# A list scheduler that keeps VectorE's SBUF operations off GpSimd's additions, with new due times and another order of products in the first full round

## The chip, the cores and the metric

One core of one Trainium2 chip. The metric is the time of one execution on the device, in microseconds; of several runs the median.

## The reference

Softcapped attention, then a feed-forward layer with an ELU between its two products. Cut to what matters:

```python
# q, k, v: (4, 12, 448, 64); cap = 30; w_in: (768, 2048), w_out: (2048, 768), both float64
scores = cap * tanh((q @ k.T / 8) / cap)
attn = exp(scores - max) / (sum + 1e-9)
x = (attn @ v).transpose(0, 2, 1, 3).reshape(1792, 768)
h = x @ w_in
g = where(h > 0, h, exp(min(h, 0)) - 1)
out = (g @ w_out).astype(float32)
```

## The kernel before, in words

The attention (Attention.run, the first 155 us) runs over 12 rounds of two pairs of heads, in an order written out by hand; the change does not touch it. Its result x stays in SBUF as 6 chunks c of 128 features by 1792 tokens.

The layers run over 8 rounds r. A round takes 256 of the 2048 hidden features, as two slices f = 2r and 2r + 1, and the tokens in four blocks t: 384, 384, 512 and 512 wide (BLOCKS, L33). Every operand is split in a high and a low part of a rounded format; a product is then three matrix multiplies (high by high, low by high, high by low: products, L398, lines L402 to L404). Names in the trace and the order: xh1_3 and xl1_3 are the two parts of block 1, chunk 3; wh7 and wl7 those of weight tile 7; h2_0 is slice 2 of block 0 in PSUM, e2_0 its ELU on the way, gh2_0 and gl2_0 the parts of the result; o0_3_2 the output of round 0, block 3, chunks 2 and 3.

Blocks 0 and 1 go through h (hidden, 18 multiplies a slice) and o (outputs, 12 multiplies for each pair of chunks, three pairs). For blocks 2 and 3 the first product of rounds 1 to 7 is not made directly: seven products m1 to m7 of half the depth (block, 9 multiplies each) take the place of eight, on sums and differences of quarters of the weights and of x ("forms"; the x ones are kept in DRAM and fetched into a ring of three SBUF slots, t1_3_0 and so on). VectorE's additions (add, L489 to L497) and ScalarE's copy (keep) put the seven together in SBUF as c1, c, u2 and u3, and each gives one h. Round 0 makes all four blocks directly.

PSUM: two single banks hold h and m in turn, three double ones ("s") hold o. A bank is free again when the operation that reads it has run: for h the bend (L435, VectorE, of the ELU: exp on ScalarE L430 and L431, bend, high part on ScalarE L445, low part on VectorE L449); for m the keep or the add; for o in round 0 the leave (ScalarE, L467), later the gather (VectorE, L472), which adds o to x.

The weights come as float64 words, one tile of 128 by 768 at a time, four tiles a round (4r and 4r + 1 for h and m, 4r + 2 and 4r + 3 for o). Weights.steps makes each one a float32 out of its bits: ScalarE L118 and L121, VectorE L129, L132 and L145, GpSimd's integer addition (L148), ScalarE's high part (L155), VectorE's low part (L159). The load of a tile into its one buffer (L106) waits for L145 of the tile before.

The order of all this is made while the program is built. Each operation is a Step with an engine, a length in us from a formula, a due time, what it needs, gives, takes and frees; steps stand in threads, and Plan.run places them one at a time: the engine that can start first, and on it, of the steps that can start then, the one with the smallest due time. TensorE's steps are one thread in a fixed order (plan_products), and Moe.clock adds up their lengths: due times are given against that clock. The result is only an order for each engine; on the chip every engine takes its list in that order and waits for semaphores.

Of the kernel before, what the change touches and what calls it, by code (L numbers as in the profile page):

```python
# [18 lines left out]
BANK = 512  # L19
# [6 lines left out]
FT = 2  # L26
# [274 lines left out]
class Step:  # L301


    def __init__(self, engine, us, due, f, *a, needs=(), gives=None, takes=None, frees=()):
        self.engine, self.us, self.due, self.f, self.a = engine, us, due, f, a
        self.needs, self.gives, self.takes, self.frees = needs, gives, takes, frees


class Plan:
# [31 lines left out]
    def run(self):  # L341

        free, order = dict(FREE), []
        heads = [[t, 0, -9.0] for t in self.threads]
        while heads:
            able = []
            for head in heads:
                step = head[0][head[1]]
                start = self.ready(step, head[2])
                if start is not None:  # L350
                    able.append((start, step, head))
            first = {}
            for start, step, head in able:
                e = step.engine
                start = start if e is None else max(start, free[e])
                first[e] = min(first.get(e, start), start)
            if not first:
                raise RuntimeError([h[0][h[1]].a for h in heads])
            engine = min(first, key=lambda e: first[e])
            now = first[engine]  # L360
            due, _, step, head = min(
                ((step.due, k, step, head) for k, (start, step, head) in enumerate(able)
                 if step.engine == engine and start <= now),
                key=lambda e: e[:2],
            )
            end = now + step.us
            if engine is not None:
                free[engine] = end
            order.append(step)
            end += LAG[engine]  # L370
            if step.takes is not None:
                kind, owner = step.takes
                self.slots[kind][1].append(None)
                self.owner[owner] = kind, len(self.slots[kind][1]) - 1
            for owner in step.frees:
                kind, k = self.owner.pop(owner)
                self.slots[kind][1][k] = end
            if step.gives is not None:
                self.known[step.gives] = end
            head[1] += 1  # L380
            if head[1] == len(head[0]):
                heads.remove(head)
            else:
                head[2] = now + step.us if head[0][head[1]].engine == engine else end
# [5 lines left out]
class Moe:  # L390
# [121 lines left out]
    def plan_elu(self, r, t, i, due, needs=(), frees=(), freed=()):  # L512
# [4 lines left out]
            Step("v", dve(width), due + 1.2, self.bend, *k, frees=frees, gives=freed or None),  # L517
            Step("s", act(width), due + 2.5, self.high, *k, takes=("g", ("g", *k))),
            Step("v", dve(width), due + 4.0, self.low, *k, frees=(("e", *k),), gives=("g", *k)),
        )  # L520

    def plan_first(self, r, t, i):
# [9 lines left out]
        self.plan_elu(r, t, i, end, needs=(("p", r, t, i),), frees=frees)  # L532

    def plan_second(self, r, t):
# [3 lines left out]
        for e in range(0, NC, 2):  # L538
            single = last and e == NC - 2
            for k in (e, e + 1) if single else (e,):  # L540
# [6 lines left out]
                if r:  # L547
                    step = Step("v", dve(n * width), end + 1.5, self.gather, r, t, k, n, needs=(key,), frees=(key,))
# [7 lines left out]
    def plan_block(self, n, r):  # L556
# [26 lines left out]
        if n == 1:  # L583
            p.thread(
                Step("s", act(BANK), end, self.keep, "c1", "m1", r, needs=(key,), frees=(key,),
# [4 lines left out]
        more = {}  # L590
        if out == "c":
            more["takes"] = "ev", ("c", r)
        elif out:
# [3 lines left out]
        add = [Step("v", dve(BANK), end, self.add, u, f"m{n}", r, out, needs=needs, gives=gives,  # L597
                    frees=() if n == 5 else (key,), **more)]
        if n == 5:
            add.append(Step("v", dve(BANK), end, self.add, "u2", "m5", r, gives=("u", "u2", r, 5), frees=(key,)))  # L600
# [3 lines left out]
        for name, t, i, ready in elu:  # L604
            got = ("got", name, r)
            p.thread(Step(None, 0.0, 0.0, self.bring, name, r, t, i, needs=(ready,), gives=got))
            self.plan_elu(r, t, i, end + 0.8, needs=(got,), frees=((name, r),))

    def plan_products(self):
# [6 lines left out]
        self.plan_elu(0, 0, 0, -2.4, needs=(("p", 0, 0, 0),))  # L616
# [6 lines left out]
        for r in range(1, NR):  # L623
            self.begun[r] = self.clock
            for n in (1, 6):
                if r == 1 and n == 1:
                    first(r, 0)
                self.plan_block(n, r)
            if r > 1:
                first(r, 0)  # L630
            self.plan_second(r - 1, 3)
            self.plan_block(7, r)
            first(r, 1)
            self.plan_second(r, 0)
# [107 lines left out]
    def run(self, normalised):  # L742
# [14 lines left out]
        for r in range(1, NR):  # L757
            start = self.begun[r]
            before = self.begun.get(r - 1, start - 56.0)
            for i in range(FT):  # L760
                self.plan_tile(2 * FT * r + i, (before + 12.0 if r > 1 else start - 24.0) + 13.0 * i)
            self.plan_forms(r, before + 34.0 if r > 1 else start - 4.0)
            for i in range(FT, 2 * FT):
                self.plan_tile(2 * FT * r + i, before + 13.0 * i + 12.0 if r > 1 else start + 10.0 * (i - 1) - 4.0)
# [3 lines left out]
class Attention:  # L768
# [225 lines left out]
    def plan_rest(self, p):  # L994
# [6 lines left out]
        def spread(k, *needs):  # L1001
# [11 lines left out]
            Step("v", 0.7, 0.0, self.take_sums, n, needs=("summed",), frees=(("sums",),)),  # L1013
            Step(None, 3.7, 0.0, None),
            Step("v", 0.32, 0.0, self.invert, n),
# [244 lines left out]
```

## Time and profile before

| | |
|---|---|
| median of 3 runs | 622.81 us (622.63 to 626.21) |
| the profiled execution's own time | 623.72 us |
| its span, first to last instruction | 621.9 us |
| TensorE (PE) busy | 608.4 us, 98% of the span |
| VectorE (DVE) busy | 491.0 us, 79% |
| ScalarE (ACT) busy | 365.3 us, 59% |
| GpSimd (POOL) busy | 63.7 us, 10% |
| TensorE's granted clock, mean | 0.997 of full speed |

Busy time is the union of an engine's instructions; a matrix multiply is shown longer than the distance to the next one, since they overlap, so distances from start to start tell TensorE's pace. A row of the timeline shows start and length in us, engine, line, operation and operands; a bracket at its end shows how long the engine was idle before it and what ended that.

### The profile page before, as it was taken

The numbers are of one execution on the slowest core, as the hardware profiler recorded it, in microseconds if no ns is written. First come the engines' busy times: TensorE is split into PE (matmuls) and PEld (weight loads), VectorE is DVE, ScalarE is ACT, GpSimd is POOL, SyncE is SP. The second block draws the span as 40 slices with busy tenths as digits, with TensorE's granted clock in tenths as the row PEclk, the third lists the DMA queues.
The fourth block names the chain that finished last, engine by engine and source line by source line (L and its number), as shares of the span: only waits on it lengthen the run. The fifth ranks groups of instructions, "written<-read, shape, count | busy, mean of one in ns | idle before, by whom it ended". The sixth has DMA issues, their size and how long they took to land.

```text
span 621.9 us, 8936 instructions
## 1 busy us (share of the span) xinstructions
PE 608.4 (98%) x3347; PEld 473.6 (76%) x3347; DVE 491.0 (79%) x684; ACT 365.3 (59%) x527; POOL 63.7 (10%) x40
## 2 busy tenths in 40 slices
PE   8999999999999989899999999999999999999996
PEld 3444444444798879788988998898889889888985
DVE  5898999997899957986895989588688959764463
ACT  6999999999866954644453544345454434431330
POOL 0010010010110122112111101111111112010000
PEclk9999999999999999999999999999999999999999
DMA  5556457462222875644544444454644445342444
GB/s 186 166 162 208 130 151 232 128 208 59 84 82 85 338 237 201 237 143 146 207 168 169 156 149 159 155 199 168 229 152 157 153 153 203 110 170 85 163 168 174
DMA packets 39622, 103.08 MB, mean 166 GB/s; under 512 B 11026, under 2 KB 15890, under 8 KB 39570
## 3 DMA queue, kind: packets, MB, share of 16 engines
q1 hardware_dynamic: 39282, 101.90, 48.0%
q8 instruction: 28, 0.46, 0.3%
q10 hardware_dynamic: 288, 0.52, 0.3%
q14 instruction: 24, 0.20, 0.1%
HBM read 90.44 MB, written 11.88 MB: 165 GB/s over the span
## 4 chain that ended last, share of the span: by engine, by line
PE 87%; DVE 7%; DMA 2%; ACT 2%; issue 1%; SPq 0%; DVEq 0%; ACTq 0%
PE o L404 11%; PE o L402 11%; PE o L403 11%; PE pv L853 10%; PE s L811 8%; PE m L402 5%; PE m L404 5%; PE m L403 5%; PE h L402 5%; PE h L403 5%; PE h L404 5%; PE sum L897 3%; PE pv L866 2%; PE s L828 1%; DVE xl L248 1%
## 5 line engine op out<-in xcount | busy, mean ns | idle before, releaser
L402 PE MATMUL o<-gh,wh 128*128 128x384 f32 (+1 forms) x380 | 138.2, 364 | 1.8 <-ACT wv L118 1.8
L404 PE MATMUL o<-gh,wl 128*128 128x384 f32 (+1 forms) x380 | 138.4, 364 | 0.0
L403 PE MATMUL o<-gl,wh 128*128 128x384 f32 (+1 forms) x380 | 138.0, 363 | 0.0
L472 DVE TENSOR_TENSOR x<-o,x 128x768 f32<-128x768 f32 (+1 forms) x83 | 89.8, 1084 | 22.6 <-PE o L404 22.0
L148 POOL TENSOR_TENSOR wv<-wv,wq 128x768 int32<-128x768 int32 x24 | 47.3, 1973 | 362.6 <-DVE wv L145 322.9
L402 PEld LDWEIGHTS o<-gh,wh 128*128 128x128 f32 x380 | 71.7, 189 | 9.9 <-ACT wv L118 2.2
L844 ACT ACTIVATE s<-s 128x896 f32<-128x896 f32 x84 | 76.6, 912 | 4.6 <-PE s L828 3.5
L846 ACT ACTIVATE p<-s 128x896 f32<-128x896 f32 x84 | 77.2, 919 | 2.7
L403 PEld LDWEIGHTS o<-gl,wh 128*128 128x128 f32 x380 | 71.7, 189 | 7.9
L404 PEld LDWEIGHTS o<-gh,wl 128*128 128x128 f32 x380 | 71.6, 189 | 7.7
L402 PE MATMUL h<-xh,wh 128*128 128x384 f32 (+1 forms) x210 | 71.4, 340 | 0.8 <-DVE e L435 0.8
L404 PE MATMUL h<-xh,wl 128*128 128x384 f32 (+1 forms) x210 | 71.2, 339 | 0.0
L403 PE MATMUL h<-xl,wh 128*128 128x384 f32 (+1 forms) x210 | 71.2, 339 | 0.0
L853 PE MATMUL pv<-p,vf 128*64 128x448 f32 x276 | 59.5, 552 | 0.0
L445 ACT ACTIVATE gh<-e 128x384 fp32r<-128x384 f32 (+1 forms) x64 | 36.0, 570 | 27.1 <-DVE e L435 27.1
L430 ACT ACTIVATE e<-h 128x384 f32<-128x384 f32 (+1 forms) x36 | 18.0, 499 | 54.8 <-PE h L404 54.7
L435 DVE SCALAR_TENSOR_TENSOR e<-e,h 128x384 f32<-128x384 f32 (+1 forms) x36 | 20.2, 564 | 34.4 <-ACT e L431 34.3
L449 DVE TENSOR_TENSOR gl<-e,gh 128x384 fp32r<-128x384 f32 (+1 forms) x64 | 41.0, 650 | 6.7 <-ACT gh L445 6.7
L402 PEld LDWEIGHTS h<-xh,wh 128*128 128x128 f32 x210 | 39.4, 188 | 3.9 <-DVE e L435 1.1
L853 PEld LDWEIGHTS pv<-p,vf 128*64 128x64 f32 x276 | 16.8, 136 | 31.0 <-issue 23.3
L403 PEld LDWEIGHTS h<-xl,wh 128*128 128x128 f32 x210 | 39.4, 188 | 1.3
L404 PEld LDWEIGHTS h<-xh,wl 128*128 128x128 f32 x210 | 39.4, 188 | 0.7
(132 smaller groups left out, 1036.5 us busy)
## 6 DMA issues: line engine op xcount, KB each, us to landing
t<-form SPq DMA_DIRECT2D x81, 512.0 KB, 5.3
pre<-in_w_dram SPq DMA_DIRECT2D x32, 768.0 KB, 5.7
raw<-in_qk_dram SPq DMA_DIRECT2D x22, 448.0 KB, 4.2
form<-t SPq DMA_DIRECT2D x12, 512.0 KB, 3.9
vf<-in_v_dram SPq DMA_DIRECT2D x23, 256.0 KB, 4.4
rb<-rec SPq DMA_DIRECT2D x48, 112.0 KB, 2.9
out_dram<-x SPq DMA_DIRECT2D x5, 512.0 KB, 2.8
out_dram<-x SPq DMA_DIRECT2D x6, 384.0 KB, 2.5
```

The costliest lines, as they stand in the source:

```text
L148: nc.gpsimd.tensor_tensor(out=vi, in0=vi, in1=q, op=ALU.add)
L402: mm(acc, wh[:, m, :], ph, start=first, stop=False)
L403: mm(acc, wh[:, m, :], pl, start=False, stop=False)
L404: mm(acc, wl[:, m, :], ph, start=False, stop=last)
L435: self.nc.vector.scalar_tensor_tensor(out=e, in0=e, scalar=-1.0, in1=self.h.pop(k), op0=ALU.add, op1=ALU.max)
L445: self.nc.scalar.activation(out=self.g[k][0], in_=self.e[k], func=AF.Copy)
L449: self.nc.vector.tensor_tensor(out=gl, in0=self.e.pop(k), in1=gh.bitcast(F32), op=ALU.subtract)
L472: self.nc.vector.tensor_tensor(out=o, in0=self.o.pop((r, t, e)), in1=o, op=ALU.add)
L811: yield lambda a=a, b=b, i=i: self.nc.tensor.matmul(s, a[o, k], b[o, :S], start=i == 0, stop=i == 2)
L844: self.nc.scalar.activation(out=s, in_=s, func=AF.Tanh, scale=self.con.tanh_scale)
L846: self.nc.scalar.activation(out=pt, in_=s, func=AF.Exp, scale=self.con.exp_scale)
L853: self.nc.tensor.matmul(out[o, :S], w[j], x[j], **flags)
```

## The change

Four things.

- Step gets a flag psum. A VectorE step without it (one on SBUF alone) and a GpSimd step exclude each other in the plan: Plan.run lets neither start before the other engine's last such step has ended (held). Steps with the flag are the bends of h, the adds that read m, the gathers, and the sums and their reciprocal. The order of instructions is all that comes of it; no wait is added to the program.
- The due times of the ELU, the adds and the keep move ahead: the exp of an h from the end of its product to 3 us before it, the bend from 1.2 us behind the exp to the same time, the high and low part from 2.5 and 4.0 to 3.0 and 4.5 us behind; adds and keep to 3 us before their product's end; the sums of the last attention round to -9.
- In round 1, o of round 0's block 3 stands ahead of m1 and m6 instead of behind them, and m7 behind h of block 1 instead of ahead of it.
- The due times of the weight tiles and of the weight forms are given against the start of their own round: the add of tiles 4r to 4r + 3 at -32, -19, +2 and +13, the forms at -14 (all 4 later in round 1).

```diff
-    def __init__(self, engine, us, due, f, *a, needs=(), gives=None, takes=None, frees=()):
+    def __init__(self, engine, us, due, f, *a, needs=(), gives=None, takes=None, frees=(), psum=False):
+        self.other = None if psum else {"v": "g", "g": "v"}.get(engine)
...
+        held = {"v": -9.0, "g": FREE["g"]}
...
-                start = start if e is None else max(start, free[e])
+                start = start if e is None else max(start, free[e], held.get(step.other, start))
...
-                 if step.engine == engine and start <= now),
+                 if step.engine == engine and max(start, held.get(step.other, start)) <= now),
...
             if engine is not None:
                 free[engine] = end
+                if step.other is not None:
+                    held[engine] = end
...
-    def plan_elu(self, r, t, i, due, needs=(), frees=(), freed=()):
+    def plan_elu(self, r, t, i, due, needs=(), frees=(), psum=True):
...
-            Step("v", dve(width), due + 1.2, self.bend, *k, frees=frees, gives=freed or None),
-            Step("s", act(width), due + 2.5, self.high, *k, takes=("g", ("g", *k))),
-            Step("v", dve(width), due + 4.0, self.low, *k, frees=(("e", *k),), gives=("g", *k)),
+            Step("v", dve(width), due, self.bend, *k, frees=frees, psum=psum),
+            Step("s", act(width), due + 3.0, self.high, *k, takes=("g", ("g", *k))),
+            Step("v", dve(width), due + 4.5, self.low, *k, frees=(("e", *k),), gives=("g", *k)),
...
-        self.plan_elu(r, t, i, end, needs=(("p", r, t, i),), frees=frees)
+        self.plan_elu(r, t, i, end - 3.0, needs=(("p", r, t, i),), frees=frees)
...
-                    step = Step("v", dve(n * width), end + 1.5, self.gather, r, t, k, n, needs=(key,), frees=(key,))
+                    step = Step("v", dve(n * width), end + 1.5, self.gather, r, t, k, n, needs=(key,), frees=(key,),
+                                psum=True)
...
-                Step("s", act(BANK), end, self.keep, "c1", "m1", r, needs=(key,), frees=(key,),
+                Step("s", act(BANK), end - 3.0, self.keep, "c1", "m1", r, needs=(key,), frees=(key,),
...
-        add = [Step("v", dve(BANK), end, self.add, u, f"m{n}", r, out, needs=needs, gives=gives,
-                    frees=() if n == 5 else (key,), **more)]
+        due = end - 3.0
+        add = [Step("v", dve(BANK), due, self.add, u, f"m{n}", r, out, needs=needs, gives=gives,
+                    frees=() if n == 5 else (key,), psum=True, **more)]
...
-            self.plan_elu(r, t, i, end + 0.8, needs=(got,), frees=((name, r),))
+            self.plan_elu(r, t, i, end, needs=(got,), frees=((name, r),), psum=False)
...
-        self.plan_elu(0, 0, 0, -2.4, needs=(("p", 0, 0, 0),))
+        self.plan_elu(0, 0, 0, -3.5, needs=(("p", 0, 0, 0),))
...
         for r in range(1, NR):
             self.begun[r] = self.clock
+            if r == 1:
+                first(r, 0)
+                self.plan_second(r - 1, 3)
             for n in (1, 6):
-                if r == 1 and n == 1:
-                    first(r, 0)
                 self.plan_block(n, r)
             if r > 1:
                 first(r, 0)
-            self.plan_second(r - 1, 3)
-            self.plan_block(7, r)
+                self.plan_second(r - 1, 3)
+                self.plan_block(7, r)
             first(r, 1)
+            if r == 1:
+                self.plan_block(7, r)
             self.plan_second(r, 0)
...
         for r in range(1, NR):
             start = self.begun[r]
-            before = self.begun.get(r - 1, start - 56.0)
-            for i in range(FT):
-                self.plan_tile(2 * FT * r + i, (before + 12.0 if r > 1 else start - 24.0) + 13.0 * i)
-            self.plan_forms(r, before + 34.0 if r > 1 else start - 4.0)
-            for i in range(FT, 2 * FT):
-                self.plan_tile(2 * FT * r + i, before + 13.0 * i + 12.0 if r > 1 else start + 10.0 * (i - 1) - 4.0)
+            first = 0 if r > 1 else 4.0
+            for i, due in enumerate((-32.0, -19.0, 2.0, 13.0)):
+                if i == FT:
+                    self.plan_forms(r, start + first - 14.0)
+                self.plan_tile(2 * FT * r + i, start + first + due)
...
-            Step("v", 0.7, 0.0, self.take_sums, n, needs=("summed",), frees=(("sums",),)),
+            Step("v", 0.7, -9.0, self.take_sums, n, needs=("summed",), frees=(("sums",),), psum=True),
             Step(None, 3.7, 0.0, None),
-            Step("v", 0.32, 0.0, self.invert, n),
+            Step("v", 0.32, 0.0, self.invert, n, psum=True),
```

How the order of instructions changes is shown at three places; behind each fence stands what moved.

First, VectorE between the attention's last tile (wv3) and block 1. num23 is a copy out of PSUM; e0_0 with h0 is the bend of the first half of h0; sums11 the last softmax sums; xl1_0 and so on the low parts of block 1. Before:

```order
L904 COPY num23_1874<-pv11_1_1822 128x448
L248 TENSOR_TENSOR xl1_0_1808<-x_123,xh1_0_1807 128x384
L248 TENSOR_TENSOR xl1_1_1810<-x_123,xh1_1_1809 128x384
L248 TENSOR_TENSOR xl1_2_1812<-x_123,xh1_2_1811 128x384
L435 SCALAR_TENSOR_TENSOR e0_0_1896<-e0_0_1896,h0_1841 128x384
L248 TENSOR_TENSOR xl1_3_1814<-x_123,xh1_3_1813 128x384
```

And in the change:

```order
L912 COPY num23_1874<-pv11_1_1822 128x448
L439 SCALAR_TENSOR_TENSOR e0_0_1896<-e0_0_1896,h0_1841 128x384
L917 TENSOR_SCALAR sums11_1909<-sum11_1876,eps_88 128x448
L248 TENSOR_TENSOR xl1_0_1808<-x_123,xh1_0_1807 128x384
L248 TENSOR_TENSOR xl1_1_1810<-x_123,xh1_1_1809 128x384
```

The bend and the sums stand ahead of the low parts now.

Second, VectorE in round 1, up to the first gather of o1_1: c1 and u2 are the sums that take in m2 and m3, wv and wl a weight tile, forms the weight forms of round 2. Before:

```order
L145 SCALAR_TENSOR_TENSOR wv10_2736<-pre_73,wv10_2736 128x768
L497 TENSOR_TENSOR c1_1_2478<-c1_1_2478,m2_1_2713 128x512
L211 TENSOR_TENSOR forms_1889<-pre_73,forms_1889 128x384
L211 TENSOR_TENSOR forms_1889<-wv9_2656,forms_1889 128x384
L211 TENSOR_TENSOR forms_1889<-pre_73,forms_1889 128x384
L435 SCALAR_TENSOR_TENSOR e2_2_2791<-e2_2_2791,c1_1_2478 128x512
L497 TENSOR_TENSOR u2_1_2515<-u2_1_2515,m3_1_2732 128x512
L449 TENSOR_TENSOR gl3_2_2771<-e3_2_2723,gh3_2_2770 128x512
L449 TENSOR_TENSOR gl2_2_2815<-e2_2_2791,gh2_2_2814 128x512
L159 TENSOR_TENSOR wl10_2810<-wv10_2736,wh10_2809 128x768
L472 TENSOR_TENSOR x_123<-o1_1_0_2752,x_123 128x2x384
```

And in the change:

```order
L145 SCALAR_TENSOR_TENSOR wv9_2701<-pre_73,wv9_2701 128x768
L501 TENSOR_TENSOR u2_1_2553<-u2_1_2553,m3_1_2726 128x512
L476 TENSOR_TENSOR x_123<-o1_1_0_2743,x_123 128x2x384
L439 SCALAR_TENSOR_TENSOR e2_2_2735<-e2_2_2735,c1_1_2530 128x512
L453 TENSOR_TENSOR gl3_2_2757<-e3_2_2716,gh3_2_2756 128x512
L159 TENSOR_TENSOR wl9_2776<-wv9_2701,wh9_2775 128x768
L453 TENSOR_TENSOR gl2_2_2781<-e2_2_2735,gh2_2_2780 128x512
```

The gather of o1_1_0 stands right behind the add of m3; tile 9 is at that place where tile 10 was, and the forms come later.

Third, ScalarE before o1_0: wh7 is the high part of weight tile 7, which o1_0 reads, x<-o0_3 are the leaves of round 0's block 3, e2_1 and e3_1 the exponentials of h2_1 and h3_1. Before:

```order
L467 ACTIVATE x_123<-o0_3_0_2500 128x2x512
L467 ACTIVATE x_123<-o0_3_2_2524 128x2x512
L155 ACTIVATE wh7_2558<-wv7_2517 128x768
L467 ACTIVATE x_123<-o0_3_4_2544 128x2x512
L118 ACTIVATE pre_73<-pre_73 128x768
L121 ACTIVATE wq8_2580<-pre_73 128x768
L430 ACTIVATE e2_1_2611<-h2_1_2576 128x384
```

And in the change:

```order
L118 ACTIVATE wv7_2555<-pre_73 128x768
L121 ACTIVATE wq7_2563<-pre_73 128x768
L434 ACTIVATE e2_1_2579<-h2_1_2544 128x384
L435 ACTIVATE e2_1_2579<-e2_1_2579 128x384
L449 ACTIVATE gh2_1_2598<-e2_1_2579 128x384
L434 ACTIVATE e3_1_2608<-h3_1_2574 128x384
L435 ACTIVATE e3_1_2608<-e3_1_2608 128x384
L155 ACTIVATE wh7_2617<-wv7_2555 128x768
```

Tile 7's first steps and its high part move behind the leaves of block 3, and the high part behind the exponentials of h3_1.

## Rows read from the trace of the kernel before

**Rows 1.** Waits of TensorE, 148 us to the end: total, times, longest (us).
```profile
PE o L402 <- ACT wv L118: 1.8, 1, 1.8
PE m L402 <- issue: 1.7, 1, 1.7
PE m L402 <- DVE e L435: 1.2, 1, 1.2
PE h L402 <- DVE e L435: 0.8, 1, 0.8
```

**Rows 2.** Timeline of TensorE around the four waits: start, length, line, operands.
```profile
162.59 0.34 PE L404 MATMUL h<-xh,wl 128*128 128x384 f32 x1
163.76 0.45 PE L402 MATMUL h<-xh,wh 128*128 128x384 f32 x1 [0.83 <-DVE e L435]
...
215.35 0.34 PE L404 MATMUL h<-xh,wl 128*128 128x384 f32 x1
216.91 0.50 PE L402 MATMUL m<-xh,wh 128*128 128x512 f32 x1 [1.21 <-DVE e L435]
...
220.98 0.47 PE L402 MATMUL m<-t,forms 128*128 128x512 f32 x1 [1.74 <-issue]
...
260.28 0.39 PE L404 MATMUL m<-t,forms 128*128 128x512 f32 x1
262.48 0.47 PE L402 MATMUL o<-gh,wh 128*128 128x512 f32 x1 [1.81 <-ACT wv L118]
...
266.43 0.40 PE L403 MATMUL o<-gl,wh 128*128 128x512 f32 x1
...
269.87 0.39 PE L403 MATMUL o<-gl,wh 128*128 128x512 f32 x1
```

**Rows 3.** Busy time by stretch; the third number from the end is the granted clock.
```profile
205.00:220.00 15.00, 13.03 (x65) 11.24 (x63) 14.54 (x23) 13.66 (x24) 2.11 (x1) 1.00 0.80 298
250.00:262.00 12.00, 10.67 (x56) 9.53 (x54) 11.83 (x18) 7.34 (x13) 1.85 (x1) 1.00 0.59 211
264.00:266.00 2.00, 2.00 (x6) 1.60 (x5) 2.00 (x4) 0.81 (x2) 0.00 (x0) 0.50 0.51 207
```

**Rows 4.** Timeline of VectorE, 218 to 262 us.
```profile
218.24 2.18 DVE L449 TENSOR_TENSOR gl<-e,gh 128x384 fp32r<-128x384 f32 x1
220.34 0.54 DVE L435 SCALAR_TENSOR_TENSOR e<-e,h 128x384 f32<-128x384 f32 x1
...
237.86 0.55 DVE L435 SCALAR_TENSOR_TENSOR e<-e,h 128x384 f32<-128x384 f32 x1 [1.46 <-ACT e L431]
...
243.12 0.56 DVE L129 TENSOR_SCALAR wv<-wv 128x768 f32<-128x768 f32 x1 [0.18 <-ACT wv L118]
...
261.39 0.95 DVE L472 TENSOR_TENSOR x<-o,x 128x768 f32<-128x768 f32 x1
```

**Rows 5.** Timeline of GpSimd: its additions at two of these places.
```profile
217.89 2.11 POOL L148 TENSOR_TENSOR wv<-wv,wq 128x768 int32<-128x768 int32 x1 [13.46 <-DVE wv L145]
...
236.55 1.85 POOL L148 TENSOR_TENSOR pre<-pre,wq 128x768 int32<-128x768 int32 x1 [8.25 <-DVE pre L145]
```

**Rows 6.** Timeline of all engines, 238 to 241 us: tile 8 and e3_1.
```profile
238.88 0.83 ACT L155 ACTIVATE wh<-pre 128x768 fp32r<-128x768 f32 x1
...
239.70 0.33 PE L402 MATMUL o<-gh,wh 128*128 128x384 f32 x1
...
239.75 0.96 DVE L159 TENSOR_TENSOR wl<-pre,wh 128x768 fp32r<-128x768 f32 x1 [0.18 <-ACT wh L155]
...
239.90 0.49 ACT L430 ACTIVATE e<-h 128x384 f32<-128x384 f32 x1 [0.18 <-PE h L404]
...
240.42 0.53 ACT L431 ACTIVATE e<-e 128x384 f32<-128x384 f32 x1
```

**Rows 7.** DMA issues of the page: KB each, median us from issue to landing.
```profile
t<-form SPq DMA_DIRECT2D x81, 512.0 KB, 5.3
pre<-in_w_dram SPq DMA_DIRECT2D x32, 768.0 KB, 5.7
```

More of the change, by code (lines that the diff above doesn't have):

```diff
@@ L596, in plan_block @@
         gives = ("u", out or u, r) if out else ("u", u, r, n)
-        add = [Step("v", dve(BANK), end, self.add, u, f"m{n}", r, out, needs=needs, gives=gives,
-                    frees=() if n == 5 else (key,), **more)]
+        due = end - 3.0
+        add = [Step("v", dve(BANK), due, self.add, u, f"m{n}", r, out, needs=needs, gives=gives,
+                    frees=() if n == 5 else (key,), psum=True, **more)]
         if n == 5:
-            add.append(Step("v", dve(BANK), end, self.add, "u2", "m5", r, gives=("u", "u2", r, 5), frees=(key,)))
+            add.append(Step("v", dve(BANK), due, self.add, "u2", "m5", r, gives=("u", "u2", r, 5), frees=(key,), psum=True))
         elu = {4: [("c", PAIR, 1, gives)], 2: [("c1", PAIR, 0, gives)],
```

## The prediction

> **What bounds the kernel now.** I read the waits of TensorE from 148 us on first. From there to the end of the span it has four waits and no other [rows 1]: 0.8, 1.2, 1.7 and 1.8 us. All four lie between 163 and 263 us, that is in the opening (round 0, all of round 1). Behind 263 us TensorE's products follow each other without a break for 350 us. So whatever the change does to VectorE or GpSimd after that is worth nothing on the credit side; it can only add waits.
>
> Next I read TensorE's own timeline at the four places, from start to start, since products overlap [rows 2]. A 512-column product starts every (269.87 - 266.43) / 15 = 0.229 us; a 384-column one, by its columns, every 0.172 us. What each place costs over that:
> - h0, second half: 163.76 - 162.59 - 0.17 = 1.0 us.
> - m1 of round 1: 216.91 - 215.35 - 0.17 = 1.4 us.
> - m6: nine steps of m1 are 2.06 us, and 220.98 - 216.91 is 4.07: 2.0 us.
> - o1_2_0: 262.48 - 260.28 - 0.23 = 2.0 us.
> - behind it, ten steps took 266.43 - 262.48 = 3.95 us where 2.29 are due: 1.7 us. [...]
>
> Sum 8.1 us. That is all that can be won, 1.3% of the profiled execution's 623.72 us.
>
> Who is late at each place is read from VectorE's timeline. At 163.76 the releaser is a bend (L435), the operation that reads an h bank. At 216.91 it is again a bend; ScalarE came late to the exponentials before it. At 220.98 the tag says "issue", but m6 takes the bank of h3_0, and that bank's bend ran at 220.34, right behind a low part that took 2.18 us instead of 0.55 [rows 4]. GpSimd's addition ran from 217.89 to 220.00 [rows 5]: the low part was held until it ended, and the bend stood behind it. At 262.48 the tag names ScalarE's wv, which ended in the same moment; o1_2_0 needs the PSUM room of o1_1_0, and that room's gather ran from 261.39 to 262.34 [rows 4]. o1_1_0's last product started about 254.2 (260.28 less eight steps of m5 and 25 of o1_1), so the gather stood 7 us in VectorE's queue, which was busy for 11.83 of the 12 us up to 262 [rows 3].
>
> **The change part by part.**
> First wait. On VectorE the bend of h0's first half moves from behind three low parts (first order) to the place behind the copy of num23. Three operations of the bend's size, at 0.55 us, are 1.6 us and more, over the 1.0 that it was late. Gone: -1.0. The sums' addition, now ahead of the low parts xl1, waits for TensorE's sums, which end before h0's second half begins; xl1_0 is wanted 18 products (3.1 us) later, and six low parts start 0.5 us apart, as fast as they are wanted. Nothing.
>
> Second and third wait. The order of products puts o0_3 (36 products of 512 columns, 8.2 us) between h3_0 and m1. The two bends now have 8.2 us before m1 and 10.3 us before m6, where they were 1.4 and 2.0 late. A low part held by GpSimd for 1.6 us no longer matters there. What o0_3 needs is early: its last low part, gl1_3, stands before the three t3 parts in VectorE's list, by my count of the queue 3 us ahead. Gone: -3.4. In exchange h2_1 now follows m6 directly and needs m1's bank, whose copy by ScalarE stands behind the three evictions of o0_3. The last of those is through while m1 still runs; then the copy waits for m1's end alone. By the 0.49 us that ScalarE needs for 384 columns [rows 6] it is some 0.7 us for 512, and it has the 2.06 us of m6 as cover. Nothing, with about a microsecond to spare. m7 moves behind h2_1 and h3_1, so its chunks, fetched when m6 lets go of them, have 6.2 us of products plus m6's rest; a fetch takes 5.3 us to land, in the median [rows 7]. Nothing, with 2 us to spare.
>
> Fourth wait. The gather of o1_1_0 moves up: tile 10's three passes and its low part, four low parts of forms and two more operations no longer stand before it (second order). It stands right behind m3's addition now, and m3 ends where o1_1 begins, so it runs as soon as o1_1_0 is done; o1_2_0 wants the room two thirds of o1_1 and m5 later (4.1 + 2.1 us). The gather of o1_1_4, behind the forms, is the tightest one, by my count of VectorE's queue half a microsecond ahead of o1_2_4. Gone: -2.0, and -1.7 with it if the low clock came from that idle stretch.
>
> [...] The rows show 1.00 granted through the idle stretches of 1.2 and 1.7 us and 0.50 right after that of 1.8 [rows 1, 3], so by rows alone the fall may or may not come from the idling. [...]
> By the rows alone: the low stretch is the only one in the opening and begins within a microsecond or two of the longest idle stretch. I take the 1.7 us as gone.
>
> New work on the path. Tile 7's high part on ScalarE now stands behind the exponentials of e3_1 (third order), which wait for h3_1; o1_0 begins one block (m7) after h3_1. With the rows of tile 8 [rows 6]: h3_1's next block starts at 239.70, the exponentials end at 240.95, 1.25 us later. High part 0.83, low part 0.96: 3.05 us after h3_1, with no gaps. o1_0 starts 2.06 us after it, and its sixth product is the first to read tile 7's low part: 2.06 + 5 x 0.172 = 2.92 us. Late by 0.1 to 0.2 us. This cost is bounded below by 0 (a stand-in that ends earlier releases nothing earlier) and above by what the worst row shows, 2.0 us idle plus 1.7 us of low clock, if tile 7 itself is late. Its load is issued only when tile 6 has been combined, by my count of the queues 7.2 us after h3_0's end. Landing 5.7 [rows 7], a ScalarE pass of 0.83 [rows 6], two VectorE passes of 0.56, a combine like the low part's 0.96, and 1.85 for GpSimd [rows 4 to 6] make 17.7 us; ScalarE is ready for the high part 8.2 + 4.1 + 6.2 + 1.25 = 19.8 us after h3_0's end, 2 us later. I take 0.2 us, nearest to the row-by-row count.
>
> Due times and holding. From round 2 on tiles start 12 to 20 us later than before (rounds are 55.7 us by their steps; start - 32, -19, +2, +13 against start - 44, -31, -18, -5). The order has no wait in it for "holding"; it only changes what stands next to an addition. An operation that reads PSUM is not held: the bend at 237.86 took 0.55 us inside an addition from 236.55 to 238.40 [rows 4, 5]. VectorE may win some 1.5 us per addition, which nothing waits for: 0 at best. At worst, the rival below.
>
> **The sum.** -1.0 - 3.4 - 2.0 - 1.7 + 0.2 = -7.9 us from 623.72. The profiled execution stands 0.9 us above the median, so I apply the difference to the median: 622.8 - 7.9 = 614.9 us.
>
> **Rivals.**
> A. One wait takes the place of the four: tile 7 (above), m7's chunks, or the gather of o1_1_4. For it: all three have 0.5 to 2 us to spare, and each hangs on a DMA or a full queue. Against it: none is negative by the rows. It costs up to 2.0 + 1.7 as at 262.48, so 614.9 + 3.6 = 618.5 us.
> B. The low clock comes although TensorE does not idle: 614.9 + 1.7 = 616.6 us. For it: two of three long idles show none. Against: the only low stretch follows the longest idle.
> C. The change does not do what it says: the planner's clock is not the chip's, additions meet SBUF operations anyway, and the queue before o1_2 stays as late as it was. Then the opening's new order alone helps: -1.0 - 3.4 + 0.2, or 618.6 us; with another wait of 2 us 620.6 us. For it: nothing in the program enforces the holding, and for tile 4 the forms' low parts still stand right behind the combine. Against: the gather's place in the order is fixed, whatever GpSimd does.
> D. Slower: late weight tiles. VectorE takes its list in order; the gather at 261.39 shows 7 us of that. Now bends and additions stand ahead of weight passes and wait for TensorE, with the tile queued behind, and o of the next round waits for the tile. For round 2, tile 11 is combined behind the gather of o1_3_0: gather 1.3 (0.95 by columns), passes 0.56 twice, a low part 0.55, combine 0.96, then 4.2 from the addition's start at 236.55 to the low part's end at 240.71 [rows 4 to 6]: 8.3 us. From o1_3_0's end to o2_0 TensorE has 24 x 0.229 + 9 x 0.229 + 36 x 0.172 = 13.8 us. It decides once the tile is 5.5 us later than that, in each of six rounds: then 2.0 + 1.7 us each, 614.9 + 22 = 637 us. [...] Against: 5.5 us are more than any VectorE row here.
>
> **How the numbers follow.** Forecast 0.60, A 0.18, B 0.08, C 0.08, D 0.06. A measurement of this kernel can tell about 1%, that is 616.6 us. Faster by more: the forecast, half of B, and some of A with short waits: 0.68. Within 1%: 0.26. Slower: D, 0.06. The likeliest case alone spans 614.0 to 616.0 (8.2 gone and nothing new, to a microsecond of new waits). For 8 in 10 the range goes up over A and C: 613.8 to 619.2 us.
>
> **What would show it.** In the changed profile, no wait over 0.3 us in TensorE's list after 148 us; at most a short one of o1_0 on tile 7's low part; granted clock 1.00 from 250 to 280 us; m1_2 starting 8 us earlier than before against the span's start; PE busy over 99% from 148 us to the last product. A wait at m7, o1_0 or o1_2_4 makes it A; 0.50 without one, B; a gather of o1_1_0 still over 5 us late, C; waits of o on wh or wl in rounds 2 to 7, D. It is wrong outright if TensorE's waits are gone and the time is not.

## The result and the profile after

The changed kernel takes 616.53 us, median of 5 runs (615.65 to 616.79); the kernel before, run beside it, 623.33 us (622.63 to 626.21). The ratio is 0.9885, 95% interval 0.9862 to 0.9908: 1.15% faster. A second set of runs gave 616.13 us and 0.9881 (0.9864 to 0.9898). Predicted were 614.9 us, 7.9 us less than before; 6.8 us less were measured. The profiled execution took 616.79 us, its span is 614.9 us: 7.0 us shorter than in the profile before.

The list of TensorE's waits from 148 us to the end, which had four rows [rows 1], is empty. The four places in TensorE's timeline, to be held against [rows 2] (lines 402 to 404 are 406 to 408 now):

```profile
162.61 0.33 PE L408 MATMUL h<-xh,wl 128*128 128x384 f32 x1
162.78 0.33 PE L406 MATMUL h<-xh,wh 128*128 128x384 f32 x1
...
223.00 0.39 PE L408 MATMUL o<-gh,wl 128*128 128x512 f32 x1
223.22 0.39 PE L406 MATMUL m<-xh,wh 128*128 128x512 f32 x1
...
225.04 0.39 PE L408 MATMUL m<-xh,wl 128*128 128x512 f32 x1
225.26 0.39 PE L406 MATMUL m<-t,forms 128*128 128x512 f32 x1
...
256.48 0.39 PE L408 MATMUL m<-t,forms 128*128 128x512 f32 x1
256.71 0.39 PE L406 MATMUL o<-gh,wh 128*128 128x512 f32 x1
```

Each step is 0.17 to 0.23 us where it had been 1.17, 1.56, 2.12 (m1's last product starts at 218.86) and 2.20. The same stretches of busy time as in [rows 3], and VectorE's gather of o1_1_0 (261.39 us before, [rows 4]):

```profile
250.00:262.00 12.00, 12.00 (x61) 10.67 (x60) 11.90 (x20) 7.40 (x13) 1.84 (x1) 1.00 0.59 200
264.00:266.00 2.00, 2.00 (x10) 1.68 (x9) 2.00 (x4) 0.00 (x0) 0.00 (x0) 1.00 0.00 0
```

```profile
250.65 0.96 DVE L476 TENSOR_TENSOR x<-o,x 128x768 f32<-128x768 f32 x1
```

The clock of 0.50 behind o1_2_0 is gone. VectorE is as full as before from 250 to 262 us (11.90 of 12), but the gather that TensorE wants now stands near the front of that queue. Over the whole span it is less busy:

```profile
PE 605.9 (99%) x3347; PEld 472.0 (77%) x3347; DVE 475.9 (77%) x684; ACT 365.1 (59%) x527; POOL 63.1 (10%) x40
```

That is 15.1 us less than the 491.0 of before for the same 684 instructions; where it comes from is shown below.

m1 of round 2 starts at 264.91 us, 272.36 before: 7.45 us earlier; the last product 7.4 us earlier (608.53 against 615.89); from there to the end of the span it is 6.4 us, 6.0 before. What is missing from the 7.9 stands among the waits of the weight loads (PEld), 150 to 260 us, since those of the products are too short to be listed:

```profile
PEld h L407 <- DVE xl L248: 0.8, 2, 0.4
...
PEld o L408 <- DVE wl L159: 0.2, 1, 0.2
```

The second is the new wait of o1_0 on tile 7, 0.2 us, as forecast. The first was not forecast. It lies in h0_2, which took 4.45 us from first to last start (177.34 to 181.79) instead of 3.9. Its low parts xl2 stood behind the addition of num23, which waits for a DMA (VectorE's timeline, the changed kernel):

```profile
177.79 0.63 DVE L941 TENSOR_TENSOR x<-num,rb 128x448 f32<-128x448 f32 x1 [1.67 <-DMA rb<-rec]
178.34 1.29 DVE L248 TENSOR_TENSOR xl<-x,xh 128x512 fp32r<-128x512 f32 x2
```

### The profile page after: what moved, and what is told of

Read it like the earlier page. It is cut to its first block, busy times and chain, and to the rows that moved or that the text cites. A ratio compares the mean times of both kernels' runs of the same rounds, so it can differ in the third digit from the quotient of the medians.

```text
span 614.9 us, 8926 instructions
## 1 busy us (share of the span) xinstructions
PE 605.9 (99%) x3347; PEld 472.0 (77%) x3347; DVE 475.9 (77%) x684; ACT 365.1 (59%) x527; POOL 63.1 (10%) x40
## 4 chain that ended last, share of the span: by engine, by line
PE 97%; ACT 1%; DMA 0%; DVE 0%; issue 0%; SPq 0%; ACTq 0%
PE o L408 12%; PE o L407 12%; PE o L406 12%; PE pv L861 10%; PE s L819 8%; PE h L407 6%; PE h L406 6%; PE h L408 6%; PE m L408 6%; PE m L407 6%; PE m L406 6%; PE sum L905 3%; PE pv L874 2%; PE s L836 2%; DMA pre<-in_qk_dram 0%; ACT p L854 0%
## 5 line engine op out<-in xcount | busy, mean ns | idle before, releaser
L439 DVE SCALAR_TENSOR_TENSOR e<-e,h 128x384 f32<-128x384 f32 (+1 forms) x36 | 20.2, 564 | 33.1 <-ACT e L435 33.1
```

What stands on the lines that cost most here:

```text
L439: self.nc.vector.scalar_tensor_tensor(out=e, in0=e, scalar=-1.0, in1=self.h.pop(k), op0=ALU.add, op1=ALU.max)
```

## The experiments

The question is which part of the change took which wait, and whether the four waits are separate costs, as the prediction added them up. Every set was run beside the kernel before on the same chip (medians 623.3 to 624.0); so the ratios are what is compared.

### One part alone, and one part taken back

**order_alone**: the kernel before with the product order alone.

```diff
         for r in range(1, NR):
             self.begun[r] = self.clock
+            if r == 1:
+                first(r, 0)
+                self.plan_second(r - 1, 3)
             for n in (1, 6):
...
```

> The kernel before with the new order of products alone (o0_3 between h3_0 and m1, m7 behind h3_1). Theory 1, the four waits are separate costs: the waits of m1 and m6 go (3.4 us), the first wait and that of o1_2_0 with its low clock stay: 623.3 - 3.4 = 619.9 us. Theory 2, the wait of o1_2_0 is set by VectorE's queue, which was busy 11.83 of 12 us ahead of it and doesn't get shorter: TensorE reaches o1_2_0 3.4 us earlier and waits 3.4 us longer there, 5.4 us instead of 2.0, and the time stays within 1 us of 623.3.

Measured: 624.45 us, ratio 1.0007 (0.9985 to 1.0029). Nothing won. Waits of TensorE, 148 us to the end, and busy time around o1_2_0, from a profiled execution of 627.55 us, the longest of the ten runs:

```profile
PE o L402 <- DVE x L472: 4.4, 1, 4.4
PE m L402 <- DMA t<-form: 2.2, 4, 1.0
PE h L402 <- DVE e L435: 0.8, 1, 0.8
```

```profile
261.00:264.00 3.00, 0.00 (x0) 0.00 (x0) 3.00 (x6) 1.93 (x5) 0.00 (x0) 0.99 0.87 246
264.00:267.00 3.00, 1.83 (x4) 1.49 (x5) 3.00 (x5) 0.81 (x2) 0.00 (x0) 0.50 0.80 325
267.00:270.00 3.00, 3.00 (x8) 2.31 (x7) 2.97 (x6) 2.56 (x5) 0.00 (x0) 0.50 0.02 7
```

The waits on bends at m1 and m6 are gone, as theory 1 wanted, but the time is that of theory 2: TensorE came earlier to o1_2_0 and stood idle from 261 to 264 us while VectorE worked all 3.00 us. The gather came at 264.08 us, even later than before, and the clock was 0.50 for almost 7 us. New are waits on fetched chunks (t from form).

VectorE's own work is not all that keeps this queue. Before the window above, VectorE itself stood idle for the weight tiles in its list (VectorE's timeline):

```profile
235.71 0.56 DVE L129 TENSOR_SCALAR pre<-pre 128x768 f32<-128x768 f32 x1 [2.59 <-ACT pre L118]
...
245.65 0.56 DVE L129 TENSOR_SCALAR wv<-wv 128x768 f32<-128x768 f32 x1 [2.05 <-ACT wv L118]
```

The loads of the tiles are issued at 228.05, 237.91 and 247.86 us, each when the tile before is combined. Tile 10's first pass on VectorE stands at 255.46 us (252.68 before), and the gather, which comes behind it in the list, follows 8.6 us later (8.7 before). As long as tile 10 stands ahead of the gather, an earlier TensorE does not make it earlier.

**tiles_alone**: the kernel before with the due times of tiles and forms alone.

```diff
-            before = self.begun.get(r - 1, start - 56.0)
...
+            first = 0 if r > 1 else 4.0
+            for i, due in enumerate((-32.0, -19.0, 2.0, 13.0)):
...
```

> The kernel before with the new due times of the weight tiles and forms alone. The gather of o1_1_0 stands nine places earlier in VectorE's list. Theory 1, separate costs: the wait of o1_2_0 goes (2.0 us) and the low clock behind it (1.7 us), the first three waits stay: 623.3 - 3.7 = 619.6 us, granted clock 1.00 from 250 to 280 us. Theory 2, the low clock is not tied to the idling: 623.3 - 2.0 = 621.3 us, with 0.50 for about 2 us somewhere between 255 and 280 us.

Measured: 619.02 us, 0.9924 (0.9902 to 0.9947), the profiled execution without a low clock: theory 1, and more, since m6 is nearly free too. Waits, and where m6's wait went, in the timelines of VectorE and GpSimd:

```profile
PE m L402 <- DVE e L435: 1.6, 1, 1.6
PE h L402 <- DVE e L435: 0.8, 1, 0.8
PE m L402 <- issue: 0.2, 1, 0.2
```

```profile
218.51 0.55 DVE L449 TENSOR_TENSOR gl<-e,gh 128x384 fp32r<-128x384 f32 x1
218.98 0.54 DVE L435 SCALAR_TENSOR_TENSOR e<-e,h 128x384 f32<-128x384 f32 x1
```

```profile
218.76 2.01 POOL L148 TENSOR_TENSOR wv<-wv,wq 128x768 int32<-128x768 int32 x1 [14.34 <-DVE wv L145]
```

The low part gl2_0 now starts 0.25 us before GpSimd's addition and takes 0.55 us, where it started 0.35 us behind it and took 2.18 [rows 4, 5]. The bend of h3_0 reads PSUM and runs beside the addition in 0.54 us.

**order_tiles**: both together on the kernel before (no diff of its own).

> The kernel before with the new order of products and the new due times of tiles and forms, without the holding and without the due times of the bends, additions and sums. Theory 1, these two carry all but the first wait: m1, m6, o1_2_0 without a wait, the first wait of 1.0 us stays, and the 0.55 us that h0_2 lost in the changed kernel does not come in: 616.5 + 0.5 = 617.0 us. Theory 2, the holding is needed at o1_2_0 or at another bank: a wait of 1 to 2 us comes back there, 618 to 620 us.

Measured: 617.34 us, 0.9887 (0.9842 to 0.9933): theory 1 in the sum. The waits are the first one and half a microsecond at m7:

```profile
PE h L402 <- DVE e L435: 0.8, 1, 0.8
PE m L402 <- DMA t<-form: 0.5, 1, 0.5
```

**bends_alone**: the kernel before with the due times of exponentials, bends, parts, sums, adds and keep.

```diff
-            Step("v", dve(width), due + 1.2, self.bend, *k, frees=frees, gives=freed or None),
+            Step("v", dve(width), due, self.bend, *k, frees=frees, psum=psum),
...
```

> The kernel before with the new due times of exponentials, bends, parts, sums and additions alone. Theory 1: the first wait goes (1.0 us); m1 and m6 wait as before (1.4 and 2.0 us) or less; at o1_2_0 TensorE arrives that much earlier and the queue of VectorE is no shorter, so that wait and the low clock grow by the same: 622 to 624 us, no difference. Theory 2, waits are separate costs: 623.4 - 1.0 or less, 619 to 622.4 us.

Measured: 624.00 us, 1.0006 (0.9989 to 1.0023), no difference. The profiled execution, 627.78 us, is the longest of the ten. Its waits, and two stretches behind them:

```profile
PE m L406 <- DVE e L439: 3.0, 1, 3.0
PE m L406 <- DMA t<-form: 2.5, 1, 2.5
PE o L406 <- ACT wv L118: 2.4, 1, 2.4
```

```profile
236.00:238.00 2.00, 2.00 (x6) 1.71 (x6) 0.63 (x2) 0.13 (x1) 0.00 (x0) 0.50 0.43 170
...
268.00:270.00 2.00, 2.00 (x10) 1.62 (x10) 2.00 (x4) 1.73 (x4) 0.00 (x0) 1.00 0.81 291
```

The first wait is gone, and so is the one at m6 (1.7 us). Those of m1 (1.2 before) and o1_2_0 (1.8 before) grew, and one of 2.5 us at m7 is new. It is theory 1, though not at o1_2_0 alone: the microsecond was lost again at m1 and m7.

**hold_alone**: the kernel before with the holding and its flags.

```diff
-                start = start if e is None else max(start, free[e])
+                start = start if e is None else max(start, free[e], held.get(step.other, start))
...
```

> The kernel before with the holding alone (all due times and the order of products old). Theory 1, it changes the order of VectorE's operations enough to help: the bend of h0 goes ahead of the low parts and the first wait is gone (1.0 us), the gather of o1_1_0 stands four operations earlier; but tile 10 still stands ahead of it: 620 to 622 us. Theory 2, as with the bends' due times alone, what goes ahead of o1_2_0 is waited for there: 623 to 624.5 us.

Measured: 623.28 us, 0.9990 (0.9971 to 1.0009): theory 2. The first wait is gone here too (in the plan a bend may go while the low parts are held), and others stand in its place, one of them new, of o0_0 on gl1_0 at 173 us:

```profile
PE o L407 <- DVE gl L453: 3.0, 2, 1.5
PE m L406 <- DVE e L439: 2.0, 1, 2.0
PE o L406 <- DVE x L476: 0.3, 1, 0.3
```

**tiles_back**: the changed kernel with the old due times of tiles and forms (the diff of tiles_alone, reversed).

> The changed kernel with the old due times of tiles and forms; the new order of products, the holding and the due times of the bends stay. Theory 1, VectorE's queue ahead of the gather of o1_1_0 is what the old due times make long: the gather ends near 262 us as before, TensorE reaches o1_2_0 near 256 us and waits 4 to 6 us, the clock falls to 0.50 behind it: 622 to 625 us, all of the gain gone. Theory 2, the holding and the earlier bends shorten that queue as well: a wait of at most 2 us, 617 to 620 us.

Measured: 623.82 us, 0.9999 (0.9985 to 1.0013): theory 1, all of the gain gone through one wait.

```profile
PE o L406 <- DVE x L476: 4.9, 1, 4.9
```

```profile
256.00:260.00 4.00, 0.05 (x1) 0.00 (x0) 4.00 (x6) 0.38 (x1) 1.96 (x1) 1.00 0.84 259
...
262.00:264.00 2.00, 2.00 (x6) 1.54 (x6) 2.00 (x3) 1.94 (x5) 0.00 (x0) 0.50 0.57 234
```

**order_back**: the changed kernel with the old product order (the diff of order_alone, reversed).

> The changed kernel with the old order of products; all due times and the holding stay. Theory 1, the new order is what gives the bends of h2_0 and h3_0 their time: waits of 1.4 us at m1 and up to 2 us at m6 come back, o1_2_0 has no wait and the clock stays at 1.00 there: 618 to 620 us. Theory 2, the earlier due times of the bends already do it: no wait over 0.3 us at m1 and m6, within 0.5 us of 616.5.

Measured: 622.22 us, 0.9966 (0.9951 to 0.9982); theory 1 in kind, but dearer: the two waits at m1 and m6 are 4.7 us, and behind the longer one the clock falls.

```profile
PE m L406 <- DVE e L439: 4.7, 2, 3.1
```

```profile
222.00:224.00 2.00, 1.83 (x4) 1.49 (x5) 1.46 (x3) 0.52 (x1) 0.84 (x1) 0.55 0.65 262
```

**hold_back**: the changed kernel with the holding taken out.

```diff
-                start = start if e is None else max(start, free[e], held.get(step.other, start))
+                start = start if e is None else max(start, free[e])
...
```

> The changed kernel with the holding taken out of the planner, all due times and the new order of products kept. Theory 1, holding is worth nothing once the order and the due times are new: 616.5 us within 0.5, no wait over 0.3 us in TensorE after 148 us, more time of VectorE beside GpSimd's additions (about 1.5 us for each that meets an operation on SBUF alone). Theory 2, holding carries a part: low parts of 1.2 to 2.4 us make a bend or a gather late, one wait of 1 to 2 us between 200 and 265 us, 617.5 to 620 us.

Measured: 616.40 us (615.71 to 617.07), 0.9873 (0.9828 to 0.9919): theory 1. No wait is listed after 148 us, and m1 of round 2 starts at 264.30 us. Holding is worth nothing here.

So the parts do not add up:

| kernel | ratio to before |
|---|---|
| product order alone | 1.0007 |
| due times of bends and adds alone | 1.0006 |
| holding alone | 0.9990 |
| due times of tiles and forms alone | 0.9924 |
| product order and tiles | 0.9887 |
| all but the holding | 0.9873 |
| all | 0.9885, 0.9881 |
| all but the product order | 0.9966 |
| all but the tiles' due times | 0.9999 |

Multiplied, the four parts alone make 0.9927; together they make 0.9885. No run has all but the due times of the bends and adds; the kernel without them and without the holding, the fifth row, can't be told from the whole.

### Where VectorE's 15 us come from

The groups of line 211 (low parts of the weight forms, 128x384) by operand, 150 to 622 us: count, busy us, mean ns. The kernel before:

```profile
L211 DVE TENSOR_TENSOR forms<-pre,forms 128x384 fp32r<-128x384 f32 x14 | 17.3, 1239 | 0.0
L211 DVE TENSOR_TENSOR forms<-wv,forms 128x384 fp32r<-128x384 f32 x14 | 12.7, 910 | 0.0
```

With the holding alone:

```profile
L211 DVE TENSOR_TENSOR forms<-pre,forms 128x384 fp32r<-128x384 f32 x14 | 17.6, 1258 | 0.0
L211 DVE TENSOR_TENSOR forms<-wv,forms 128x384 fp32r<-128x384 f32 x14 | 9.8, 697 | 0.0
```

With the tiles' due times alone:

```profile
L211 DVE TENSOR_TENSOR forms<-wv,forms 128x384 fp32r<-128x384 f32 x14 | 9.1, 649 | 0.7 <-ACT forms L207 0.7
L211 DVE TENSOR_TENSOR forms<-pre,forms 128x384 fp32r<-128x384 f32 x14 | 7.7, 550 | 0.2 <-ACT forms L207 0.2
```

An undisturbed one takes 0.55 us, and in the changed kernel all 28 do: 7.7 us for each group, 15.4 where it was 30.0. With the old due times they stand one operation behind a tile's combine (L145), which releases GpSimd's addition, and one or two of them a round end only 0.4 us behind its end: in the kernel before one ran from 300.23 to 302.44 us, the addition from 300.02 to 302.03. The plan with the holding places them elsewhere on paper, yet on the chip they meet all the same. I counted VectorE's operations behind 150 us that run beside an addition and take over 0.45 us more than the median of their kind: 16 in the kernel before, with 20.2 us too much in all; 9 (12.9 us) with the holding alone, 11 (15.8 us) in tiles_back, which has the holding too; 4 (5.1 us) in tiles_alone, 5 (5.8 us) in hold_back, 5 (5.1 us) in the changed kernel. From 20.2 to 5.1 are the 15.1 us. VectorE's whole busy time from 150 us on agrees: 357.0 us before, 342.2 with the tiles' due times alone, 341.9 in the changed kernel and 342.3 without its holding, but 352.7 with the holding alone and 355.2 in tiles_back. So the due times of the tiles and forms do nearly all of it, and the holding beside them next to nothing. None of those counted reads PSUM, and both inputs of each lie in SBUF. In the kernel before, the 28 low parts of the forms show it: 11 of them stood beside an addition and took 1.56 to 2.21 us, an undisturbed one 0.55. The gathers, the adds that read m and the bends of h also ran beside additions there, and none of them is among the 16; the bend of h3_0, in tiles_alone above, took 0.54 us.

### The half microsecond in h0_2

**split_earlier**: the changed kernel with the low parts xl2 due earlier.

```diff
-            self.plan_split(2, c, 8.0 + 0.7 * c)
+            self.plan_split(2, c, 5.0 + 0.7 * c)
```

> The changed kernel with the low parts xl2 due 3 us earlier, so that those of the third and fourth chunk stand ahead of the additions of the last two heads (num22, num23), which wait for a DMA. Theory 1, the 0.55 us that h0_2 lost came from these parts behind the additions: h0_2 takes 3.9 us instead of 4.45, m1 of round 2 starts 0.5 to 0.6 us earlier, 616.0 us. Theory 2, the loss has another cause or comes back at the next bank: h0_2 or the products behind it as late as now, 616.5 us.

**changed_again**: the changed kernel, no edit.

> The changed kernel once more, as what the two kernels with a late gather are compared with on the same chip: 616.5 us within 0.6, granted clock 1.00 from 250 to 270 us.

Measured: split_earlier 615.95 us (615.59 to 616.24), h0_2 3.9 us, m1 of round 2 at 264.48, as theory 1 had it. But changed_again, without any edit, gave 616.13 us (615.47 to 616.41), and its profiled execution has h0_2 at 3.9 us and m1 of round 2 at 264.27. VectorE's timeline there:

```profile
176.90 0.63 DVE L941 TENSOR_TENSOR x<-num,rb 128x448 f32<-128x448 f32 x1 [1.35 <-DMA rb<-rec]
177.44 1.29 DVE L248 TENSOR_TENSOR xl<-x,xh 128x512 fp32r<-128x512 f32 x2
```

The same instructions ran 0.9 us earlier, because the chain of small DMAs ahead of them came in earlier: the reciprocal, which waits for the first of them, started at 167.06 us instead of 167.74, and the two additions that wait for later ones at 172.25 instead of 172.82 and at 176.90 instead of 177.79. So the loss is real where it occurs (in order_back h0_2 took 4.41 us), it comes in some executions and not in others, and nothing shows that the edit pays: split_earlier and the changed kernel can't be told apart.

### The idle stretch and the clock

**late_short** and **late_long**: the changed kernel with one more need for the gather of o1_1_0, to make TensorE idle at o1_2_0 by a chosen length: the end of m5 in late_short, as in the diff, the second addition of m5 in late_long.

```diff
+                    more = (("m", 5, 1),) if (r, t, k) == (1, 1, 0) else ()
-                    step = Step("v", dve(n * width), end + 1.5, self.gather, r, t, k, n, needs=(key,), frees=(key,),
+                    step = Step("v", dve(n * width), end + 1.5, self.gather, r, t, k, n, needs=(key, *more), frees=(key,),
```

> The changed kernel with the gather of o1_1_0 told to wait for the end of m5, which puts it behind that of o1_1_2 in VectorE's list; nothing else is late. By the rows of the changed kernel the gather ends near 257.9 us and o1_2_0, at 256.7 now, starts 1.2 us later. Theory 1, the clock falls only behind a longer idle stretch (1.8 us in the kernel before): the time is 1.2 us more, 617.7 us, granted clock 1.00. Theory 2, the clock falls at this place for another reason: 0.50 for about 2 us or more, 619 to 620 us.

> The same with the gather of o1_1_0 told to wait for the second addition of m5 as well. The gather ends near 259.5 us and o1_2_0 starts 2.9 us later than in the changed kernel. Theory 1, the idle stretch brings the low clock back: 2.9 us and 1.7 to 2.7 us for the clock, 621.1 to 622.1 us, 0.50 granted behind 259 us. Theory 2, the clock is not tied to the idling: 619.4 us, 1.00 granted.

Measured: 616.92 us (616.13 to 617.69) and 617.17 us (616.07 to 618.00), against 616.13 beside them. Neither theory was put to the test, since the idle stretch did not come. In late_long (TensorE, then VectorE):

```profile
257.42 0.47 PE L406 MATMUL o<-gh,wh 128*128 128x512 f32 x1 [0.80 <-DVE x L476]
```

```profile
256.32 0.95 DVE L476 TENSOR_TENSOR x<-o,x 128x768 f32<-128x768 f32 x1
...
258.85 0.95 DVE L476 TENSOR_TENSOR x<-o,x 128x768 f32<-128x768 f32 x1
```

o1_2_0 started before the late gather (258.85) had begun, so it took another room: that of o1_1_2, whose gather now ran first and ended at 257.27. In this program a room is taken in the order of release, not in turn as I had assumed. It waited 0.8 us, and the clock stayed at 1.00.

On the clock the other kernels say more. In the profiled executions the granted clock of the layers, up to 300 us, stays at 1.00 behind every idle stretch of TensorE of up to 1.7 us, and falls to 0.50 during or up to 1.2 us behind those of 1.8 (before), 2.5 and 3.0 (bends_alone), 3.1 (order_back), 4.4 (order_alone) and 4.9 us (tiles_back). It did not fall behind 2.0 us in hold_alone (m1) and 2.4 us in bends_alone (o1_2_0, the second window shown there). None of the kernels whose stretches are all under 1.8 us has a low clock there: changed kernel, hold_back, tiles_alone, order_tiles, split_earlier, late_short, late_long. So the low clock was seen only with long stretches, but the length of one stretch alone does not decide it.

## Why the prediction was right, and where it was not

**What can be won, 8.1 us.** Right. The four waits, with the low clock behind the last, were all there was; with none left the products of round 2 start 7.45 us earlier in one execution and 8.1 us (272.36 to 264.27) in the other. The time fell by 6.8 and 7.8 us in the two sets of medians (623.33 to 616.53, 623.96 to 616.13).

**First wait, "Gone: -1.0".** Right: it is in order_tiles (0.8 listed), gone in the changed kernel and in hold_back. The step beside it failed, that for the sums' addition ahead of the low parts: "Nothing". With it the reciprocal moved ahead, which waits for its DMA until 167.74 us, and the bend of h0's second half and the addition of num19, at 168.40 (166.09 before), stand behind it; the next DMAs take their buffers from that addition. The order also put xl2's third and fourth low part behind num23. That cost 0.55 us in one of the two profiled executions of the changed kernel: the mis-sized term of the sum. The holding has a part in it: in hold_back, with the same due times, num19 stands ahead of the reciprocal (165.67 and 166.81 us), num23's addition runs at 175.94 us, and h0_2 takes 3.9 us.

**Second and third wait, "-3.4", and the fourth, "-2.0".** The total is right, the division among the edits is wrong. The prediction gave the 3.4 us to the product order, as if they could be had alone; alone it was worth nothing (1.0007). What it frees is waited for at o1_2_0, because VectorE's queue ahead of the gather, tile 10 in it, is no shorter. The prediction had the numbers for it: 11.83 of 12 us busy, and a gather 7 us late. It read 2.0 us as the price of that queue, when it was only what was left after TensorE had already lost 4.4 us further up. That the sum still came out is owed to the change having both parts at once; in that much it was luck. Rival C, which gave the new order, with the queue as late as it was, 618.6 us, falls by the same error. The due times of the tiles are the part without which nothing is won (0.9999), and they take m6's wait as well, by setting gl2_0 ahead of GpSimd's addition, if only by 0.25 us, which nobody had forecast. The product order is then worth 0.0037 (0.9924 to 0.9887), some 2 us (the intervals overlap, but every run of order_tiles, up to 617.92 us, is below every run of tiles_alone, from 618.34 us), and taking it back from the changed kernel costs 5 us (0.9966 against 0.9881).

**The clock, "-1.7".** Right: the low stretch behind o1_2_0 went with the wait, in the profile of every kernel that lacks the wait, so rival B is out. That it would go was my estimate, from the one low stretch (0.50 from 264 to 266 us [rows 3]) behind the longest idle stretch; what lowers the clock is not shown. Of the idle stretches from 1.8 to 2.5 us some came with a low stretch and some did not, and the runs leave open why. Nor does it come in every execution of the kernel before: the profiled one has a mean clock of 0.997, and six of the 57 runs beside the experiments have 0.998 or more, at 621.99 to 622.97 us. So the 1.7 us are the price in the profiled execution, not in all of them.

**New wait of o1_0, +0.2.** Right, 0.2 us.

**Costed at nothing.** h2_1's bank and the gather of o1_1_4: no wait. m7's chunks: no wait, but the cover of 2 us hangs on SP's queue. In order_tiles a weight load is issued between the second chunk and the third, in order_alone between the first and the second (SP, DMA issues):

```profile
226.66 1.02 SPq L294 DMA_DIRECT2D t<-form  x2
227.99 0.33 SPq L106 DMA_DIRECT2D pre<-in_w_dram  x1
```

There m7 waited 0.5 and up to 1.0 us. In the changed kernel that load is issued at 230.96, behind all three chunks. In tiles_back and hold_back, where the load is also issued behind all three, m7 does not wait either; no edit tested this order by itself. So rival A stood close by.

**Due times and holding, "which nothing waits for".** Right for the holding, and for VectorE's 15.1 us behind 263 us; too little for the tiles' due times, by the above. Behind 263 us no wait appeared, and none of rival D's late weight tiles: rounds 2 to 7 run at the pace of before (343.6 us from m1 of round 2 to the last product, 343.5 before). Two sums of the rivals are off, without effect: the price of A, 2.0 + 1.7, is 3.7 us and not 3.6, and the terms of tile 11 in D make 8.1 us and not 8.3, so its margin was 5.7 us.

## What to carry to other kernels

Waits that follow each other on an engine fed by another engine's in-order queue are not separate prices. Before adding them up, ask of each edit alone whether the queue gets shorter, or only the consumer earlier, and what the queue itself waits for (here the loads of the weight tiles). If only the consumer gets earlier, the next wait grows by what was won, and the clock behind it may cost more than before: in order_alone o1_2_0 waited 4.4 us instead of 1.8, and the clock behind it was 0.50 for almost 7 us.

An edit that measures as nothing alone may be worth 0.4 to 0.9% beside others; take parts back from the whole as well as trying them alone. And an order that keeps two engines apart in a plan need not do so on the chip (with the holding alone 9 of VectorE's operations still ran long beside an addition, 12.9 us too much in all); look at the durations there.

## What was not expected of the hardware

An idle stretch of 2.0 or 2.4 us left the clock at 1.00 where one of 1.8 us was followed by 0.50. The kernel with the low stretch of almost 7 us also scatters more: of ten runs of order_alone the four with a mean granted clock of 0.992 took 625.48 to 627.55 us, the other six, at 0.995 to 0.997, 622.91 to 624.67 us, while the nine runs of the changed kernel lie between 615.47 and 616.79 us. The clock is not the only source of scatter: tiles_alone, at 0.996 to 0.999 and without a low stretch in its profile, spans 618.34 to 621.44 us.
